# A linear-attention block with an MLP on one core: the first two tiles normalised in halves, and the ones column set in the normalised tiles

## The chip, the cores and the metric

The kernel runs on one core of one Trainium2 chip. A core has five engines with a queue each: TensorE (PE in the profile; PEld is its loading of weights, which overlaps the matmuls), VectorE (DVE), ScalarE (ACT), GpSimd (POOL) and SyncE (SP), which here issues all the DMA transfers. Each engine works through its own queue in order, and waits on semaphores for what the others produce. The metric is the device time in microseconds, the median of several runs; one execution was also profiled.

## The reference

All data is float32: 2048 tokens of 512 features, 32 heads of 16, a hidden layer of 1376.

```
xn  = (x - mean(x)) / sqrt(var(x) + 1e-5)
q, k, v = split(xn @ wqkv)                 # 32 heads
phi(t) = where(t > 0, t + 1, exp(t)) + 1e-6
kv  = sum over tokens of phi(k)^T v        # one 16 x 16 matrix per head
z   = sum over tokens of phi(k)
o   = phi(q) kv / (phi(q) z + 1e-6)
out = x + o @ wo + relu(xn @ w1 + b1)^2 @ w2 + b2
```

## The kernel before

The 2048 tokens are 16 tiles of 128. Every float32 product is made of three matmuls on numbers split into a high part (a copy in the matmul type, made by ScalarE) and a low part (the rest, by subtraction): high x high, high x low, low x high.

The work comes in stages. First, for each tile: statistics (`statistics`: `bn_stats` and `bn_aggr` on VectorE), the inverse root of the variance (`roots`: a logarithm and an exponential on ScalarE, then three small Newton instructions on VectorE at the head of `normalise`, lines 234 to 236), and the normalised tile `xp` (line 242). Tiles 0 to 7 are turned by TensorE (`turned_pe`, four 128 x 128 transposes into one bank); tiles 8 to 15 are regrouped by 32 small DMA transfers (`regroup`, `moves`) and turned by VectorE. The turned tile is split (`transposed` returns `high` on ScalarE, `low` on VectorE and `keep_t`, which stores tiles 0 to 7 for later), and the keys are projected with the weights `wk`, which are loaded in four parts of 128 rows and split by `heads_k` (ScalarE) and `rests_k`.

The keys go through `phi_k`, and `parts` splits the result into `pk`. The normalised tile itself is split by `tokens` into `tok`: high by ScalarE, low by GpSimd (line 116). Then `kx(i)` adds tok^T pk to four banks, twelve matmuls of 512 columns per tile: first the high-high products of the four column blocks, then high-low, then low-high, for tiles 0 to 7. The last column of the normalised tile isn't needed (the rows of a normalised tile sum to zero, so the value weights are taken less their last row), and it is overwritten with ones, so that the last row of the sum is z. In the kernel before, GpSimd does that after the split: line 314 copies a one and a zero from `consts` into the last column of the high and of the low part of `tok`.

After this stage come queries, attention, and the two layers of the MLP, which the change doesn't touch.

The schedule is manual: each engine's queue holds its instructions in the order in which the program text issues them, and only the semaphores between engines are found automatically. The start is written out by hand from line 479 on: statistics and roots of tiles 0 and 1, normalisation of tile 0, weight part 0, the turning of tile 0, weight part 1, normalisation of tile 1, a one-element GpSimd copy (line 490) that makes the load of tiles 4 to 7 wait for tile 1's factor, and so on; then the order of the projection's steps for tiles 0 and 1 (`some` does the products with the high weights, `rest` those with the low weights). From line 602 a loop goes over tiles 2 to 15: in iteration i come the projection of tile i, the turning of tile i + 1, `phi_k(i)`, `parts(i)`, `tokens(i + 1)` and `kx(i - 1)`. Ahead of the first tile stand eleven small matmuls on zeros in TensorE's queue (line 453).

The lines that set the order around the change:

```
two_tiles = statistics(0), statistics(1)
for t in two_tiles:
    roots(*t)
normalise(*two_tiles[0])
heads_k(0)
high, low, keep0 = transposed(0)
high()
heads_k(1)
normalise(*two_tiles[1])
```

Of the kernel before, what the change touches and what calls it, by code (L numbers as in the profile page):

```python
# [7 lines left out]
F32 = mybir.dt.float32  # L8
F32R = mybir.dt.float32r
AF = mybir.ActivationFunctionType  # L10
OP = mybir.AluOpType
AX = mybir.AxisListType

P = 128
# [4 lines left out]
def kernel(  # L19
# [29 lines left out]
    nc = tc.nc  # L49
    xf = x.rearrange("b s d -> (b s) d")  # L50
    of = out.rearrange("b s d -> (b s) d")
    S, D = xf.shape
    F = w1.shape[1]
    NT = S // P
    NJ = D // P
# [4 lines left out]
    NPE = 2 * TB  # L60
# [8 lines left out]
    keep = ctx.enter_context(tc.tile_pool(name="keep", bufs=1))  # L69
# [5 lines left out]
    def bank(name, tag="ps"):  # L75
        return psum.tile([P, 512], F32, name=name, tag=tag)

    def w512(name, tag, bufs):
        return work.tile([P, 512], F32, name=name, tag=tag, bufs=bufs)
# [8 lines left out]
    def two(name):  # L88
        return keep.tile([P, 2, 512], F32, name=name, tag=next_tag("x"))

    def four(name, tag, dt=F32, pool=None):
        return (pool or work).tile([P, TB, 512], dt, name=name, tag=tag)

    def pair(name):
        return keep.tile([P, 2, 512], F32R, name=name, tag=next_tag("pair"))

    def f32(ap):
        return ap.bitcast(F32)

    def gjc(ap):  # L100

        return ap.rearrange("p (j g c) -> p g j c", j=NJ, g=NJ)
# [3 lines left out]
    def copy(eng, o, i, bias=0.0):  # L106
        if eng == "act":
            nc.scalar.activation(o, i, AF.Copy, bias=bias)  # L108
        elif bias:
            ENG[eng].tensor_scalar(o, i, bias, None, op0=OP.add)  # L110
        else:
            ENG[eng].tensor_copy(o, i)

    def split(h, l, src, eh, el):
        copy(eh, h, src)
        ENG[el].tensor_tensor(out=l, in0=src, in1=f32(h), op=OP.subtract)  # L116
# [14 lines left out]
    def both(name, tags, dt=F32R, pool=keep):  # L131
        return [pool.tile([P, NJ, D], dt, name=f"{name}{u}", tag=t) for u, t in zip("hl", tags)]

    wk = both("wk", ("A0", "A1"))
# [11 lines left out]
    heads = work.tile([P, P], F32, name="heads", tag="heads")  # L146
    b1s = keep.tile([P, NF], F32, name="b1s")
    zb = keep.tile([P, D], F32, name="zb")
    consts = keep.tile([P, 3, 1], F32R, name="consts")
    one_zero, eps = consts[:, :2], f32(consts[:, 2])  # L150

    xr, xp, xg, tok, pk, kp = {}, {}, {}, {}, {}, {}

# [53 lines left out]
    def group(*tiles):  # L207
        return tiles, *(small.tile([P, 3, k], F32, name=f"{n}{tiles[0]}", tag=n) for n, k in (("st", 6), ("mv", 2), ("y", 3)))

    def measure(g, *ks):  # L210

        tiles, st, mv, _ = g
        for k in ks or range(len(tiles)):
            nc.vector.bn_stats(st[:, k, :], xr[tiles[k]])  # L214
            nc.vector.bn_aggr(mv[:, k, :], st[:, k, :])

    def statistics(*tiles):
        g = group(*tiles)
        measure(g)
        return g  # L220

    def roots(tiles, st, mv, y):

        n = len(tiles)
        nc.scalar.activation(y[:, 1, :n], mv[:, :n, 1], AF.Ln, bias=eps)
        nc.scalar.activation(y[:, 0, :n], y[:, 1, :n], AF.Exp, scale=-0.5)

    def normalise(tiles, st, mv, y):

        n = len(tiles)  # L230
        var = mv[:, :n, 1]
        y0, u, r = (y[:, k, :n] for k in range(3))

        nc.vector.scalar_tensor_tensor(u, var, 1e-5, y0, op0=OP.add, op1=OP.mult)
        nc.vector.scalar_tensor_tensor(u, u, -0.5, y0, op0=OP.mult, op1=OP.mult)
        nc.vector.scalar_tensor_tensor(r, u, 1.5, y0, op0=OP.add, op1=OP.mult)
        for k, i in enumerate(tiles):
            o, src = xp[i], xr[i]
            if i >= NPE:

                o, src = o.rearrange("p g (j c) -> p g j c", j=NJ), gjc(src)
            nc.vector.tensor_scalar(o, src, mv[:, k, 0:1], r[:, k:k + 1], op0=OP.subtract, op1=OP.mult)  # L242
            if i in groups:
                regroup(*groups[i])

    def regroup(src, G):

        for r in range(NJ):
            for g in range(NJ):
                moves.append((G[32 * g:32 * (g + 1), r], src[32 * r:32 * (r + 1), g]))  # L250
        return G
# [8 lines left out]
    def turn(o, G):  # L260

        nc.vector.transpose(o.rearrange("p j (r t) -> p r j t", r=NJ),  # L262
                            G.rearrange("p r (j c) -> p r j c", j=NJ))

    def slot(i):
        return slice((i % TB) * P, (i % TB + 1) * P)

    def cols(i):

        return xsb[(i // TB + 1) % 2]  # L270

    def turned_pe(i):
        p = bank(f"pt{i}", "acc" if i < 3 else "ps")
        for j in range(NJ):
            at_j = slice(j * P, (j + 1) * P)
            nc.tensor.transpose(p[:, at_j], xp[i][:, at_j], ident)  # L276
        return p.rearrange("p (j t) -> p j t", j=NJ)

    def transposed(i, t=None):

        b, at = i // TB, slot(i)
        if i < NPE:
            t = t or turned_pe(i)
        else:
            t = xT[b][:, :, at]
            turn(t, xg[i])
        h, l = (x[:, :, at] for x in cols(i))

        def high():
            nc.scalar.activation(h, t, AF.Copy)  # L290

        def low():
            nc.vector.tensor_tensor(out=l, in0=t, in1=f32(h), op=OP.subtract)

        def keep_t():
            if i < NPE:
                k = w512(f"t{i}", "p", 6).rearrange("p (j t) -> p j t", j=NJ)
                copy("act", k, t)
                nc.sync.dma_start(xTd[b][:, :, at], k)

        return high, low, keep_t

    def run(*what):
        for f in what:
            f()

    def tokens(i):
        tok[i] = pair(f"tok{i}")
        h, l = tok[i][:, 0], tok[i][:, 1]
        src = xp[i]  # L310
        if i >= NPE:
            h, l, src = gjc(h), gjc(l), src.rearrange("p g (j c) -> p g j c", j=NJ)
        split(h, l, src, "act", "pool")
        nc.gpsimd.tensor_copy(tok[i][:, :, D - 1:], one_zero)  # L314

    def phi(ps, p, mid=lambda: None, late=lambda: None):

# [6 lines left out]
    def project(i, ps, w, steps, first=True, last=True):  # L324

        for n, (j, u, v) in enumerate(steps):
            nc.tensor.matmul(ps, lhsT=cols(i)[u][:, j, slot(i)], rhs=w[v][:, j, :], start=first and n == 0,  # L327
                             stop=last and n == len(steps) - 1)
# [99 lines left out]
    t, rk = two("x0"), four("rk", "r0")  # L428
    for i in range(2):
        load_x(i, t[:, i:i + 1])  # L430
    def load_k(*js):
        for j in js:
# [4 lines left out]
    nc.gpsimd.memset(ident, 0.0)  # L437
    nc.gpsimd.affine_select(out=ident, in_=ident, compare_op=OP.not_equal, fill=1.0, base=0,
                            pattern=[[-1, P]], channel_multiplier=1)
    nc.gpsimd.memset(f32(one_zero[:, 0]), 1.0)  # L440
    nc.gpsimd.memset(f32(one_zero[:, 1]), 0.0)
    nc.gpsimd.memset(heads, 1.0)
    h3 = heads.rearrange("p (h d) -> p h d", d=D // H)
    for sign, base in ((1, 0), (-1, D // H - 1)):
# [25 lines left out]
    def heads_k(*js):  # L470
        for j in js:
            copy("act", wk[0][:, j, :], rk[:, j])
# [4 lines left out]


    pks = [bank(f"pk{i}") for i in range(3)]
    two_tiles = statistics(0), statistics(1)  # L480
    for t in two_tiles:
        roots(*t)
    normalise(*two_tiles[0])
    heads_k(0)
    high, low, keep0 = transposed(0)
    high()
    heads_k(1)
    normalise(*two_tiles[1])

    nc.gpsimd.tensor_copy(x4[:, 0, :1], two_tiles[1][3][:, 2, :1])  # L490
    load_x(4, x4)
# [10 lines left out]
    keep1()  # L502
    rests_k("dve", 1)
    normalise(*third)
    rests_k("dve", 3)
    fourth = statistics(3)

    def some(i, u, js, first=False):
        project(i, pks[i], wk, [(j, u, 0) for j in js], first, False)

    def rest(j):
        for i in range(2):
            project(i, pks[i], wk, [(j, 0, 1)], False, j == NJ - 1)

    for j in (0, 1):
        some(0, 0, (j,), j == 0)
    some(0, 1, (0, 1))
    some(1, 0, (0, 1), True)
    some(0, 0, (2,))
    some(0, 1, (2,))  # L520
    some(1, 0, (2,))
    some(1, 1, (0, 1, 2))
    for i in range(2):
        for u in range(2):
            some(i, u, (3,))
    rest(0)
    rest(2)
    high, low, keep2 = transposed(2)
    high()
    low()  # L530
    rest(1)
    rest(3)
    load_x(8, x8[:, :2])
# [5 lines left out]
    phi_k(0, pks[0])  # L539
    measure(soon, 0)  # L540
    tokens(0)
    parts(0)
    keep2()
    roots(*fourth)
    normalise(*fourth)
    phi_k(1, pks[1])
    measure(soon, 1)
    tokens(1)
    parts(1)
    measure(soon, 2)  # L550
# [51 lines left out]
    for i in range(2, NT):  # L602
# [12 lines left out]
        k = NPE if i + 1 == NPE else i + 2  # L615
# [13 lines left out]
        if i == 2:  # L629
            tokens(2)  # L630
# [108 lines left out]
    for n in range(2):  # L739
# [212 lines left out]
        f = NF - 2  # L952
# [31 lines left out]
        for e, f in enumerate(waiting[:-2]):  # L984
# [7 lines left out]
            if e:  # L992
                do(w2next, 2)
                if e + 8 < NF:
                    g = waiting[e + 8]
# [65 lines left out]
```

## Time and profile before

| | |
|---|---|
| median of 3 runs | 425.09 us (425.08 to 425.21) |
| the profiled execution | 425.03 us, its span 423.3 us |
| granted TensorE clock | 1.000 |
| busy: TensorE, VectorE, ScalarE, GpSimd | 417.3, 299.0, 248.6, 33.3 us |
| TensorE's wait for its first transposes after the warm-up | 0.8 us |
| weight loads of `kx` waiting for line 314 | 1.0 us in two waits |

The span is the time from the first to the last instruction; what a run takes lies 1.7 us above it. A row of the timeline or of the chain begins with the start and the duration in microseconds; then come engine, line, operation, and the tile written "<-" the tiles read. A bracket at the end is the idle time of the engine before the instruction and what ended it. Matmuls are pipelined: a row's duration is longer than the distance to the next. Rows that merge several instructions give their count (x4).

### The profile page before, as it was taken

What the parts mean: (1) busy time and instruction counts of PE and PEld (TensorE: products, weight loads), DVE (VectorE), ACT (ScalarE), POOL (GpSimd) and SP (SyncE); (2) the same over time, 40 slices, a digit from 0 to 9 for tenths busy, and PEclk for the clock granted to TensorE, in tenths of its full rate; (3) what the DMA queues carried; (4) which work ended last, traced back from release to release, by engine and by line L of the source; (5) the groups of instructions that cost most, each with busy time, mean ns of one, the idle gap of its engine ahead of it and who ended that gap; (6) DMA issues with size and microseconds to landing.
All of it is one profiled execution on the core that took longest, in us unless ns stands there. A gap on an engine that the chain in (4) does not pass through costs nothing.

```text
span 423.3 us, 5387 instructions
## 1 busy us (share of the span) xinstructions
PE 417.3 (99%) x1868; PEld 344.0 (81%) x1868; DVE 299.0 (71%) x537; ACT 248.6 (59%) x441; POOL 33.3 (8%) x52
## 2 busy tenths in 40 slices
PE   7999999999999999999999999999999999999996
PEld 6788888888887888888888888888888888888885
DVE  6897788855678877777579475586967667677253
ACT  5766667645467777565438362666667665537140
POOL 3342333330000000000000000000000000000000
PEclk9999999999999999999999999999999999999999
DMA  7853437000412231547014652501120654023602
GB/s 251 274 159 83 106 104 228 18 0 2 112 50 71 80 91 35 197 79 272 0 37 125 189 193 80 140 0 50 51 74 25 200 101 150 0 93 87 162 0 99
DMA packets 42754, 43.02 MB, mean 102 GB/s; under 512 B 5828, under 2 KB 28612, under 8 KB 42472
## 3 DMA queue, kind: packets, MB, share of 16 engines
q1 hardware_dynamic: 42728, 42.69, 33.9%
q8 instruction: 14, 0.23, 0.2%
q14 instruction: 12, 0.10, 0.1%
HBM read 30.09 MB, written 6.29 MB: 86 GB/s over the span
## 4 chain that ended last, share of the span: by engine, by line
PE 97%; DVE 1%; DMA 1%; POOL 0%; ACT 0%; issue 0%; POOLq 0%
PE acc L127 39%; PE b L411 23%; PE kx L346 10%; PE pq L327 10%; PE pk L327 10%; PE pz L127 1%; PE b L127 1%; PE pkv L722 1%; PE pt L276 1%; PE pm L127 1%; DMA x<-in_A_x_dram 1%; PE end L127 0%; DVE st L214 0%; POOL tok L116 0%; DVE xp L242 0%; ACT k L320 0%
## 5 line engine op out<-in xcount | busy, mean ns | idle before, releaser
L127 PE MATMUL acc<-w2r,s 128*128 128x512 f32 x498 | 116.6, 389 | 0.0
L127 PEld LDWEIGHTS acc<-w2r,s 128*128 128x128 f32 x498 | 93.5, 188 | 19.6
L411 PE MATMUL b<-T,aop 128*128 128x512 f32 x240 | 59.6, 389 | 0.0
L411 PEld LDWEIGHTS b<-T,aop 128*128 128x128 f32 x240 | 45.0, 188 | 9.4
L346 PE MATMUL kx<-pk,tok 128*128 128x512 f32 x192 | 47.3, 394 | 0.1
L346 PEld LDWEIGHTS kx<-pk,tok 128*128 128x128 f32 x192 | 35.4, 188 | 8.2 <-POOL tok L314 1.0
L127 PE MATMUL acc<-mh,aT 128*128 128x512 f32 x128 | 41.0, 396 | 0.0
L127 PEld LDWEIGHTS acc<-mh,aT 128*128 128x128 f32 x128 | 24.0, 188 | 5.7
L119 DVE TENSOR_TENSOR w2r<-r,w2r 128x512 fp32r<-128x512 f32 x32 | 21.9, 684 | 7.2 <-ACT w2r L108 6.4
L411 PE MATMUL b<-xs0h,aop 128*128 128x512 f32 x80 | 26.4, 391 | 0.0
L116 POOL TENSOR_TENSOR tok<-xp,tok 128x512 fp32r<-128x512 f32 x16 | 22.1, 1380 | 53.6 <-ACT tok L108 53.6
L116 DVE TENSOR_TENSOR s<-c,s 128x512 fp32r<-128x512 f32 x20 | 13.9, 693 | 16.7 <-ACT s L108 16.7
L127 PE MATMUL acc<-ml,aT 128*128 128x512 f32 x64 | 25.3, 395 | 0.0
L108 ACT ACTIVATE w2r<-r 128x512 fp32r<-128x512 f32 x32 | 20.0, 624 | 9.0 <-PE acc L127 8.7
L199 POOL MEMSET r<- 32x512 f32 x3 | 1.6, 522 | 279.1 <-DMA g<-q 145.1
L322 DVE SCALAR_TENSOR_TENSOR q<-pq,q 128x512 f32<-128x512 f32 x16 | 11.0, 689 | 17.0 <-ACT q L320 17.0
L852 DVE TENSOR_TENSOR res<-acc,res 128x512 f32<-128x512 f32 x16 | 11.0, 692 | 14.8 <-PE acc L127 14.8
L108 ACT ACTIVATE aop<-S 128x512 fp32r<-128x512 f32 x20 | 12.6, 629 | 14.6 <-DVE S L651 9.4
L318 ACT ACTIVATE q<-pq 128x512 f32<-128x512 f32 x16 | 9.5, 591 | 19.7 <-PE pq L327 19.7
L108 ACT ACTIVATE aT<-at 128x512 fp32r<-128x512 f32 x16 | 9.9, 631 | 17.3 <-DVE at L262 17.3
L318 ACT ACTIVATE k<-pk 128x512 f32<-128x512 f32 x16 | 9.5, 594 | 16.6 <-PE pk L327 16.5
L411 PEld LDWEIGHTS b<-xs0h,aop 128*128 128x128 f32 x80 | 15.0, 188 | 3.4 <-ACT rz L399 0.3
(184 smaller groups left out, 816.5 us busy)
## 6 DMA issues: line engine op xcount, KB each, us to landing
r<-in_B_w_dram SPq DMA_DIRECT2D x49, 256.0 KB, 3.0
res<-in_A_x_dram SPq DMA_DIRECT2D x8, 512.0 KB, 5.3
g<-q SPq DMA_DIRECT2D x64, 64.0 KB, 2.1
out_dram<-res SPq DMA_DIRECT2D x15, 256.0 KB, 2.0
x<-in_A_x_dram SPq DMA_DIRECT2D x5, 512.0 KB, 4.8
xTd<-t SPq DMA_DIRECT2D x8, 256.0 KB, 3.1
rq<-in_A_wqkv_dram SPq DMA_DIRECT2D x8, 256.0 KB, 5.8
xg<-xp SPq DMA_DIRECT2D x32, 64.0 KB, 2.0
```

The source lines that it names most:

```text
L108: nc.scalar.activation(o, i, AF.Copy, bias=bias)
L116: ENG[el].tensor_tensor(out=l, in0=src, in1=f32(h), op=OP.subtract)
L119: nc.vector.tensor_tensor(out=l, in0=src, in1=f32(h), op=OP.subtract)
L127: nc.tensor.matmul(ps, lhsT=a[u], rhs=b[v], start=first and n == 0, stop=last and n == 2)
L276: nc.tensor.transpose(p[:, at_j], xp[i][:, at_j], ident)
L318: nc.scalar.activation(p, ps, AF.Relu, scale=-1.0)
L322: nc.vector.scalar_tensor_tensor(p, ps, 0.0, p, op0=OP.max, op1=OP.add)
L327: nc.tensor.matmul(ps, lhsT=cols(i)[u][:, j, slot(i)], rhs=w[v][:, j, :], start=first and n == 0, stop=last and n == len(steps) - 1)
L346: nc.tensor.matmul(kxp[c], lhsT=tok[i][:, u, c * P:(c + 1) * P], rhs=pk[i][:, v], start=i == 0 and (u, v) == first, stop=i == NT - 1 and ( ...
L411: nc.tensor.matmul(ps, lhsT=a[u][:, j * P:(j + 1) * P], rhs=b[v][:, j, :], start=first and j == 0 and n == 0, stop=last and j == 1 and n == 2,
L722: nc.tensor.matmul(ps[:, at], lhsT=wvs[:, c, at], rhs=kxs[c // 2][:, c % 2, at], start=c == 0 and j == 0, stop=c == NJ - 1 and j == NJ - 1 ...
L852: nc.vector.tensor_tensor(out=r[:, a:z], in0=ps, in1=r[:, a:z], op=OP.add)
```

## The change

- Tiles 0 and 1 are no longer normalised by `normalise`. `first_roots` computes -0.5 (var + 1e-5) on VectorE as soon as the variance is there, and issues the logarithm and the exponential; `first_norm` then needs two small Newton instructions instead of three, and normalises the tile in two instructions of 256 columns each instead of one of 512.
- VectorE's order becomes: statistics of tile 0, its half factor, `bn_stats` of tile 1, the Newton steps and halves of tile 0, `bn_aggr` of tile 1, its half factor, and later its Newton steps and halves. Before, all statistics came first.
- ScalarE's order becomes: roots of tile 0, weight part 0, roots of tile 1, high part of tile 0, weight part 1. Before, both roots came ahead of weight part 0.
- TensorE does the first product of tile 0 (weight part 0) between the transposes of tile 0 and those of tile 1, instead of after both.
- The ones are written into `xp` by a GpSimd memset of one column (`ones`): for tiles 0 to 7 directly after the tile's transposes, for tiles 8 to 15 at the end of `tokens` of the tile before. The copy after the split and the tile `consts`, with its two memsets at the start, are gone; `eps` gets a tile of its own.

```diff
-    consts = keep.tile([P, 3, 1], F32R, name="consts")
-    one_zero, eps = consts[:, :2], f32(consts[:, 2])
+    eps = keep.tile([P, 1], F32, name="eps")
...
+    def first_roots(g):
+        u = keep.tile([P, 1], F32, name=f"half{g[0][0]}")
+        nc.vector.tensor_scalar(u, g[2][:, 0, 1:], 1e-5, -0.5, op0=OP.add, op1=OP.mult)
+        roots(*g)
+        return u
+
+    def first_norm(g, u):
+
+        (i,), st, mv, y = g
+        y0, t, r = y[:, 0, :1], y[:, 1, :1], y[:, 2, :1]
+        nc.vector.scalar_tensor_tensor(t, u, y0, y0, op0=OP.mult, op1=OP.mult)
+        nc.vector.scalar_tensor_tensor(r, t, 1.5, y0, op0=OP.add, op1=OP.mult)
+        for k in range(2):
+            at = slice(k * D // 2, (k + 1) * D // 2)
+            nc.vector.tensor_scalar(xp[i][:, at], xr[i][:, at], mv[:, 0, :1], r, op0=OP.subtract, op1=OP.mult)
...
             nc.tensor.transpose(p[:, at_j], xp[i][:, at_j], ident)
+        ones(i)
         return p.rearrange("p (j t) -> p j t", j=NJ)
...
+    def ones(i):
+
+        nc.gpsimd.memset(xp[i][:, D - 1:] if i < NPE else xp[i][:, NJ - 1, P - 1:], 1.0)
+
...
         split(h, l, src, "act", "pool")
-        nc.gpsimd.tensor_copy(tok[i][:, :, D - 1:], one_zero)
+        if NPE <= i + 1 < NT:
+            ones(i + 1)
...
-    nc.gpsimd.memset(f32(one_zero[:, 0]), 1.0)
-    nc.gpsimd.memset(f32(one_zero[:, 1]), 0.0)
...
-    two_tiles = statistics(0), statistics(1)
-    for t in two_tiles:
-        roots(*t)
-    normalise(*two_tiles[0])
...
+    two_tiles = group(0), group(1)
+    measure(two_tiles[0])
+    half = first_roots(two_tiles[0])
+    nc.vector.bn_stats(two_tiles[1][1][:, 0, :], xr[1])
+    first_norm(two_tiles[0], half)
+    nc.vector.bn_aggr(two_tiles[1][2][:, 0, :], two_tiles[1][1][:, 0, :])
     heads_k(0)
+    half = first_roots(two_tiles[1])
     high, low, keep0 = transposed(0)
     high()
     heads_k(1)
-    normalise(*two_tiles[1])
+    some(0, 0, (0,), True)
+    first_norm(two_tiles[1], half)
...
-    for j in (0, 1):
-        some(0, 0, (j,), j == 0)
+    some(0, 0, (1,))
     some(0, 1, (0, 1))
     some(1, 0, (0, 1), True)
     some(0, 0, (2,))
```

More of the change, by code (lines that the diff above doesn't have):

```diff
@@ L479, with some, rest @@
     pks = [bank(f"pk{i}") for i in range(3)]
-    two_tiles = statistics(0), statistics(1)
-    for t in two_tiles:
-        roots(*t)
-    normalise(*two_tiles[0])
+    def some(i, u, js, first=False):
+        project(i, pks[i], wk, [(j, u, 0) for j in js], first, False)
+    def rest(j):
+        for i in range(2):
+            project(i, pks[i], wk, [(j, 0, 1)], False, j == NJ - 1)
+    two_tiles = group(0), group(1)
[4 more added lines that the diff above has]
+    nc.vector.bn_aggr(two_tiles[1][2][:, 0, :], two_tiles[1][1][:, 0, :])
     heads_k(0)
+    half = first_roots(two_tiles[1])
     high, low, keep0 = transposed(0)
@@ L506 @@
     fourth = statistics(3)
[L508 to L513, printed above, removed]
-    for j in (0, 1):
-        some(0, 0, (j,), j == 0)
+    some(0, 0, (1,))
     some(0, 1, (0, 1))
```

## The prediction

> **What bounds the kernel now.** First the page's busy times and chain, to see which engine sets the end; then the chain in order of time, to see where that engine is not yet dense; then the timelines of VectorE, ScalarE and GpSimd over the first 24 us, because everything that the diff touches lies there.
>
> ```profile
> PE 417.3 (99%) x1868; PEld 344.0 (81%) x1868; DVE 299.0 (71%) x537; ACT 248.6 (59%) x441; POOL 33.3 (8%) x52
> PE 97%; DVE 1%; DMA 1%; POOL 0%; ACT 0%; issue 0%; POOLq 0%
> ```
>
> TensorE is busy 417.3 of 423.3 us and makes 97% of the chain. The change removes no matmul, so it can only alter when the dense stream begins and how long it is held up before it runs without a gap. The chain shows where that is:
>
> ```profile
> 7.42 0.65 PE pt L276 x4
> 8.07 0.23 PE pk L327
> ...
> 8.31 4.62 PE pk L327 x19
> 12.93 0.44 PE pt L276 x4
> ...
> 14.10 0.61 ACT k L318
> ...
> 15.96 1.30 POOL tok L116
> ...
> 17.32 0.54 POOL tok L314
> ...
> 17.91 2.34 PE kx L346 x9
> 20.25 0.44 PE pt L276 x4
> 20.68 3.01 PE kx L346 x12
> 23.69 2.72 PE pk L327 x12
> ```
>
> From 23.69 on, twelve matmuls take 2.72 us, 0.227 each, and this repeats: the stream is dense. Before that there are three losses. (1) The 19 matmuls from 8.31 end at 12.93; 19 x 0.227 = 4.31, so the first of them really ran at 8.62, 0.3 behind its weight load (a load that waits exposes about 0.3 us; it starts 0.06 after what it waited for, here a weight part that ended at 8.25, quoted below). Counting back from 12.93, the products of these twenty started at: third (first low part of tile 0) 8.84, fifth (first of tile 1) 9.30, seventh (first with weight part 2) 9.75. (2) The first kx: nine matmuls from 17.91 take 2.34 instead of 2.04. (3) The second kx: 3.01 instead of 2.72. Whatever the new code makes of these is the whole effect; the profiled execution took 425.03 us (span 423.3 and 1.7 around it), the median is 425.09.
>
> **The change, part by part: the first tiles.** The rows of VectorE, ScalarE and the loads that set the start:
>
> ```profile
> 4.33 0.18 DVE L215 BATCH_NORM_AGGREGATE mv<-st 128x2 f32<-128x6 f32 x1
> 4.43 0.67 DVE L214 BATCH_NORM_STATS2 st<-x 128x6 f32<-128x512 f32 x1
> ...
> 5.23 0.13 DVE L234 SCALAR_TENSOR_TENSOR y<-mv,y 128x1 f32<-128x1 f32 x1
> ...
> 5.58 0.16 DVE L236 SCALAR_TENSOR_TENSOR y<-y 128x1 f32<-128x1 f32 x1
> 5.78 0.55 DVE L242 TENSOR_SCALAR xp<-x,mv,y 128x512 f32<-128x512 f32 x1
> 6.24 0.15 DVE L234 SCALAR_TENSOR_TENSOR y<-mv,y 128x1 f32<-128x1 f32 x1
> ...
> 6.82 0.55 DVE L242 TENSOR_SCALAR xp<-x,mv,y 128x512 f32<-128x512 f32 x1
> 7.77 0.69 DVE L293 TENSOR_TENSOR xs1l<-pt,xs1h 128x512 fp32r<-128x512 f32 x1 [0.41 <-ACT xs1h L290]
> ```
> ```profile
> 5.35 0.29 ACT L225 ACTIVATE y<-mv,consts 128x1 f32<-128x1 f32 x1 [0.27 <-DVE y L234]
> 5.67 0.20 ACT L226 ACTIVATE y<-y 128x1 f32<-128x1 f32 x1
> 5.79 0.61 ACT L108 ACTIVATE wkh<-rk 128x512 fp32r<-128x512 f32 x1
> 7.14 0.60 ACT L290 ACTIVATE xs1h<-pt 128x512 fp32r<-128x512 f32 x1 [0.74 <-PE pt L276]
> 7.63 0.62 ACT L108 ACTIVATE wkh<-rk 128x512 fp32r<-128x512 f32 x1
> 8.15 0.59 ACT L290 ACTIVATE xs1h<-pt 128x512 fp32r<-128x512 f32 x1
> 8.63 1.15 ACT L108 ACTIVATE wkh<-rk 128x512 fp32r<-128x512 f32 x2
> ```
> ```profile
> L367 DVE TENSOR_SCALAR den<-den 128x32 f32<-128x32 f32 x16 | 2.9, 181 | 0.6
> ```
> ```profile
> 1.72 1.85 SPq L433 DMA_DIRECT2D rk<-in_A_wqkv_dram  x4
> ```
> ```profile
> DMA to landing us min/median/max: 3.7/3.7/3.7
> ```
>
> Pitch: an instruction that depends on the one before starts 0.02 to 0.04 after its end; one that doesn't starts about 0.09 before that end (5.78 + 0.55 = 6.33, the next at 6.24). A half of the normalisation (128x256) has no row. Bounds: half the elements at one per 1.04 ns leave 0.28; a doubled rate, which the 0.46 us from 5.78 to 6.24 speaks for (less than 512 x 1.04 ns), leaves 0.41. I take 0.35, on the line between the same operation over 32 columns (0.18) and over 512 (0.55).
>
> By the Trainium skill, "VectorE: DVE Perf Modes", section "Side-by-side", such an operation in fp32 moves two elements a cycle behind about 150 cycles: an estimate of 0.29 for a half, with which the end would be 424.6. The same rule gives 0.42 for the whole, where this trace has 0.55; so the trace decides.
>
> Tile 0. The half factor, 0.14, goes between the two statistics: 4.53 to 4.67, second statistics 4.59 to 5.26, the two remaining Newton steps 5.18 to 5.53, first half 5.57 to 5.92, second 5.83 to 6.18 (whole before: 6.33). The last two of four transposes are left behind the second half; four take 0.44, so 0.2 drops out of the 0.70 from the end at 7.37 to 8.07: transposes done at 6.68 instead of about 7.1.
>
> Tile 1 pays. Its aggregate now stands behind tile 0's halves: 6.09 to 6.27 instead of 5.13. The logarithm and the exponential follow (0.04 later, then 0.32 + 0.20): 6.31 to 6.83. The weight part now ahead of them, landing at 1.72 + 3.7 = 5.42, runs 5.46 to 6.07 and is out of the way. The high part of tile 0 starts 6.75 instead of 7.14. On VectorE: Newton steps 6.87 to 7.22, halves 7.26 to 7.61 and 7.52 to 7.87, against 7.37 before: 0.50 later. Transposes done 7.87 + 0.70 - 0.2 = 8.37 (8.07 before); the product moved ahead of them needs the high part of tile 0 (7.35) and is done in the gap. High part of tile 1: 8.41 to 9.01. Its first product: load 9.07, run 9.36, against 9.30: +0.06. Weight part 2 starts 0.48 after that high part: 8.89 to 9.50, load 9.56, run 9.85, against 9.75: +0.10. The low part of tile 0 starts 7.79, level with 7.77. So the early start of tile 0 isn't kept, and the stream is 0.10 late: term one, +0.10, between -0.10 (half 0.28) and +0.35 (half 0.41).
>
> **The ones.** Rows of the kx stage:
>
> ```profile
> 16.82 0.98 DVE L335 SCALAR_TENSOR_TENSOR pk<-k,pk 128x512 fp32r<-128x512 f32 x1
> ...
> 20.26 0.98 DVE L335 SCALAR_TENSOR_TENSOR pk<-k,pk 128x512 fp32r<-128x512 f32 x1
> ```
> ```profile
> 1.33 0.10 POOL L440 MEMSET consts<- 128x1 f32 x1
> ...
> 17.32 0.53 POOL L314 CAST tok<-consts 128x2 fp32r<-128x2 f32 x1
> 19.41 1.29 POOL L116 TENSOR_TENSOR tok<-xp,tok 128x512 fp32r<-128x512 f32 x1 [1.55 <-ACT tok L108]
> ```
> ```profile
> 17.91 1.91 PEld L346 LDWEIGHTS kx<-pk,tok 128*128 128x128 f32 x9 [0.56 <-POOL tok L314]
> ...
> 21.35 1.92 PEld L346 LDWEIGHTS kx<-pk,tok 128*128 128x128 f32 x9 [0.40 <-POOL tok L314]
> ```
>
> Three weight loads of each early kx pass, the fourth waits for the copy of the ones column: its columns end with that column. Without the copy the fourth waits for nothing new; the fifth is the first that reads the low part of pk, which ends at 17.80 and 21.24, just 0.05 to 0.06 before the copy did. So the wait doesn't vanish: it moves one matmul on. Per kx that is 0.227 + 0.05 = 0.28 saved. It isn't saved twice: the second kx hangs on the chain that ends at 21.24, which starts from the projection's end at 14.10 and runs through ScalarE, VectorE and GpSimd whatever the first kx did. Term two: -0.28 by 23.69. The ends are 0, if some other operand ties, and -0.79, both waits (0.5 and 0.29) gone.
>
> Why the low part doesn't come sooner: it takes 0.98 instead of the 0.69 that its kind takes elsewhere, and ends 0.54 after GpSimd's subtraction (17.26 and 20.70) both times, so the subtraction holds it, not the copy. The Trainium skill, "SBUF — State Buffer", section "Who interferes with whom", has an exclusive lock here, the second to issue blocking fully; by it the copy waited for VectorE and its removal frees nothing there, as the equal 0.54 shows. Were it shared instead, the low part would end some 0.1 earlier and the sum would be -0.28 for the whole change.
>
> Costed at nothing: sixteen one-column memsets on GpSimd, 0.1 each like those removed at the start (0.10 at 1.33), hidden because GpSimd is busy 8%; without that cover the first subtraction would be 0.1 late, and the low part with it. For tiles 3 to 7 each stands behind its tile's transposes and ahead of its own subtraction, for tiles 8 to 15 behind the regrouping loads, more than an iteration ahead of use. The other fourteen copies: their kx were dense, nothing to gain. The load of tiles 4 to 7 hangs on a GpSimd copy of tile 1's factor, which is 0.44 later and has a memset before it; SyncE's order is kept, and the tiles are first read after 16.
>
> Sum: +0.10 - 0.28 = -0.18; 425.03 - 0.18 = 424.85, with the median 0.06 above the profiled execution **424.9**.
>
> **Rivals.**
>
> ```profile
> 6.93 0.48 POOL L490 COPY x<-y 128x1 f32<-128x1 f32 x1 [4.31 <-DVE y L236]
> ```
> ```profile
> L314 POOL CAST tok<-consts x16: 187/396/534, 17.3 to 92.9; 128x2 fp32r<-128x2 f32 x16
> ```
>
> Slower: GpSimd's copy gets between tile 1's halves. Before, it issued 0.11 after the normalisation began, took 0.48 where a copy of two columns takes 0.19 at best, and ended with it: it was held. Now there is an end of the first half to slip into, at 7.61; the second half would run 7.80 to 8.15, 0.28 later, and the stream with it: 0.10 + 0.28 - 0.28 = +0.10, about 425.2, or 425.5 with halves of 0.41. It decides from a second half that ends past 8.05. Against it: the second half is queued first. 0.20.
>
> No gain in kx: another operand ties at the fourth load, so only term one is left: 425.2. For it: the low part of pk was only 0.05 ahead; against: the fourth matmul doesn't read it. 0.10.
>
> Both kx waits vanish and tile 1 isn't late: -0.79 - 0.35 = 423.9. It needs the low part of pk 0.3 sooner; the equal 0.54 speaks against. 0.09.
>
> Weight part 0 lands late: ScalarE now waits for it ahead of tile 1's logarithm. It decides past 5.8 (row: 5.42), and each microsecond then costs one; before, at 5.79, it was there without a wait. 426 would need a landing at 6.8. 0.06.
>
> **How the numbers follow.** My forecast, between 424.3 and 425.0, has 0.55. The range 424.3 to 425.5 holds it and the rivals at 425.2. What two runs of this kernel can tell apart is about 0.2%, 0.85 us: faster by that (under 424.2) only the third rival, 0.09; slower (over 425.9) the last, 0.06; the rest, 0.85, is the same.
>
> **What would show it.** Right: the halves of the second tile end near 7.9, later than 7.37; ScalarE's second high part starts near 8.4; the fifth kx load, not the fourth, is held, by VectorE's L335-line instruction; the subtraction is followed by no copy; TensorE dense 0.2 earlier than 23.69. Wrong: a half outside 0.28 to 0.41, GpSimd's copy between the halves, or kx passing without a wait.

## The result and the profile after

| | before | after |
|---|---|---|
| median | 425.13 us (424.78 to 425.54, 19 runs) | 425.94 us (425.71 to 426.35, 19 runs) |
| ratio after / before | | 1.0018, 95% interval 1.0012 to 1.0025 |
| the profiled execution: time, span | 425.03, 423.3 us | 425.71, 423.6 us |
| median span; median time outside the span | 423.5; 1.72 us (33 further runs, median 425.19) | 423.9; 2.08 us |

The change costs 0.81 us, where the prediction had a gain of about 0.2. The gain in `kx` came as forecast; the start cost much more than priced; and 0.36 us lies outside the span, which the prediction had taken as constant. The profiled execution of the kernel after is one of its shortest: its spans go from 423.6 to 424.2.

From the page of the kernel after, the busy times and the chain by engine:

```profile
PE 418.2 (99%) x1868; PEld 345.3 (82%) x1868; DVE 299.6 (71%) x539; ACT 248.3 (59%) x441; POOL 28.4 (7%) x50
PE 99%; DVE 0%; ACT 0%; issue 0%
```

The same 1868 matmuls; GpSimd is busy 4.9 us less, since memsets of 1.5 us stand in place of copies of 5.8 us and some others got shorter or went. TensorE now has 99% of the chain, but not because it is denser: the chain goes back through the warm-up (below). The chain of the kernel after in order of time, up to the end of the second `kx`:

```profile
2.97 3.63 PE warm L472 x17
6.60 0.49 PE pt L291 x4
7.09 0.02 issue
7.11 0.61 ACT xs1h L306
7.71 0.04 issue
7.76 0.50 PE pk L348
8.26 0.44 PE pt L291 x4
8.69 4.70 PE pk L348 x19
...
17.52 2.93 PE kx L367 x12
20.45 0.44 PE pt L291 x4
20.88 2.99 PE kx L367 x12
23.87 0.23 PE pk L348
```

Read the middle. The warm-up lasts to 6.60 here (before, to 5.62) and holds tile 0's transposes, whose tile is ready at 6.13; they end at 7.09, ScalarE makes the high part, the product moved ahead follows at 7.76, and tile 1's transposes start only when that product ends, at 8.26. They end at 8.69; before, at 8.07, although here the first tile landed 0.26 us earlier (first statistics at 3.34; before, 3.60). VectorE, ScalarE and TensorE's weight loads at the start of the kernel after (start, duration, then what; the bracket is idle time and what ended it):

```profile
5.39 0.74 DVE L241 TENSOR_SCALAR xp<-x,mv,y 128x256 f32<-128x256 f32 x2
6.04 0.18 DVE L511 BATCH_NORM_AGGREGATE mv<-st 128x2 f32<-128x6 f32 x1
6.25 0.15 DVE L229 TENSOR_SCALAR half<-mv 128x1 f32<-128x1 f32 x1
6.87 0.22 DVE L237 SCALAR_TENSOR_TENSOR y<-half,y 128x1 f32<-128x1 f32 x1 [0.47 <-ACT y L225]
7.32 0.73 DVE L241 TENSOR_SCALAR xp<-x,mv,y 128x256 f32<-128x256 f32 x2
```
```profile
5.79 0.63 ACT L108 ACTIVATE wkh<-rk 128x512 fp32r<-128x512 f32 x1 [0.97 <-DMA rk<-in_A_wqkv_dram]
6.33 0.28 ACT L224 ACTIVATE y<-mv,eps 128x1 f32<-128x1 f32 x1
8.73 0.60 ACT L306 ACTIVATE xs1h<-pt 128x512 fp32r<-128x512 f32 x1 [0.50 <-PE pt L291]
```
```profile
7.76 0.19 PEld L348 LDWEIGHTS pk<-wkh,xs1h 128*128 128x128 f32 x1 [0.93 <-ACT xs1h L306]
7.89 0.56 PEld L291 LDWEIGHTS pt<-ident,xp 128*128 128x128 f32 x4
...
9.38 0.30 PEld L348 LDWEIGHTS pk<-wkh,xs1h 128*128 128x128 f32 x2 [0.37 <-ACT xs1h L306]
...
17.27 0.76 PEld L367 LDWEIGHTS kx<-pk,tok 128*128 128x128 f32 x4 [0.18 <-ACT pk L108]
18.33 1.69 PEld L367 LDWEIGHTS kx<-pk,tok 128*128 128x128 f32 x8 [0.30 <-DVE pk L356]
...
20.71 0.76 PEld L367 LDWEIGHTS kx<-pk,tok 128*128 128x128 f32 x4
21.75 1.69 PEld L367 LDWEIGHTS kx<-pk,tok 128*128 128x128 f32 x8 [0.28 <-DVE pk L356]
```

Two halves take 0.73 to 0.74, where the one instruction took 0.55: 0.41 each, 0.33 apart. Tile 1 is normalised at 8.05, 4.71 after the first statistics began; before, 7.37 and 3.77. And in the last four rows each `kx` has four weight loads and is held at the fifth, by VectorE's low part of `pk`, just as forecast. That low part takes as long as before (0.98):

```profile
17.29 0.99 DVE L356 SCALAR_TENSOR_TENSOR pk<-k,pk 128x512 fp32r<-128x512 f32 x1
...
20.73 0.97 DVE L356 SCALAR_TENSOR_TENSOR pk<-k,pk 128x512 fp32r<-128x512 f32 x1
```

### The profile page after: what moved, and what is told of

The parts are those of the page before. It is cut to its first block, busy times and chain, and to the rows that moved or that the text cites. A ratio compares the mean times of both kernels' runs of the same rounds, so it can differ in the third digit from the quotient of the medians.

```text
span 423.6 us, 5383 instructions
## 1 busy us (share of the span) xinstructions
PE 418.2 (99%) x1868; PEld 345.3 (82%) x1868; DVE 299.6 (71%) x539; ACT 248.3 (59%) x441; POOL 28.4 (7%) x50
## 4 chain that ended last, share of the span: by engine, by line
PE 99%; DVE 0%; ACT 0%; issue 0%
PE acc L127 39%; PE b L432 23%; PE pk L348 10%; PE kx L367 10%; PE pq L348 10%; PE pz L127 1%; PE b L127 1%; PE warm L472 1%; PE pkv L744 1%; PE pt L291 1%; PE pm L127 1%; PE end L127 0%; ACT xs1h L306 0%; DVE zb L447 0%; DVE res L874 0%
```

## The experiments

Each kernel ran beside runs of the kernel before on the same chip, whose medians were 425.19 (for ones alone, start alone, statistics first, whole normalisation), 425.27 (product behind, both undone, warm-up of 8, no new tiles) and 425.11 (the memsets and the order of `kx`). None changes what is computed. The median span of these three sets of the kernel before was 423.5, 423.6 and 423.4, so spans from different sets compare to some 0.2. "Outside" is the time less the span.

| kernel | median, us | ratio to before, 95% interval | median span | outside | records in VectorE's queue |
|---|---|---|---|---|---|
| before | 425.13 | | 423.5 | 1.72 | 689 |
| after | 425.94 | 1.0012 to 1.0025 | 423.9 | 2.08 | 696 |
| ones alone | 424.94 | 0.9982 to 0.9999 | 423.2 | 1.73 | 692 |
| start alone | 425.94 | 1.0014 to 1.0038 | 424.25 | 1.70 | 693 |
| after, statistics first | 425.83 | 1.0006 to 1.0023 | 423.9 | 1.97 | 694 |
| after, whole normalisation | 425.73 | 1.0000 to 1.0018 | 423.8 | 1.95 | 694 |
| after, product behind | 425.80 | 1.0005 to 1.0023 | 423.7 | 2.08 | 696 |
| after, statistics first and product behind | 425.37 | 0.9992 to 1.0011 | 423.4 | 1.94 | 694 |
| ones, warm-up of 8 | 425.57 | 0.9993 to 1.0011 | 423.9 | 1.71 | 692 |
| after, no new tiles | 425.84 | 1.0004 to 1.0021 | 423.8 | 2.06 | 696 |
| ones, 2 memsets more | 424.95 | 0.9982 to 1.0000 | 423.0 | 1.955 | 694 |
| ones, 4 memsets more | 425.18 | 0.9988 to 1.0007 | 423.1 | 2.065 | 696 |
| ones, 20 memsets more | 425.09 | 0.9989 to 1.0007 | 423.4 | 1.695 | 712 |
| ones, other order of `kx` | 424.83 | 0.9980 to 0.9997 | 423.1 | 1.73 | 692 |

(The last column counts all records of VectorE's queue in the trace, with the waits and register instructions that the page leaves out.)

**The two parts apart.** The theory: the ones give their 0.28 and the start costs more than 0.10. The rival: the ones gave nothing, or less. (The edits here and below are cut short. This one is against the kernel before; the others are against the kernel after, or against the ones alone where the text says so.)

```diff
+    def ones(i):
+        nc.gpsimd.memset(xp[i][:, D - 1:] if i < NPE else xp[i][:, NJ - 1, P - 1:], 1.0)
...
-        nc.gpsimd.tensor_copy(tok[i][:, :, D - 1:], one_zero)
+        if NPE <= i + 1 < NT:
+            ones(i + 1)
```

> The kernel before with the ones part alone: the memsets in the normalised tiles in place of the copies after the split; the start is that of before. Theory A (the loss lies in the start, the ones are a gain): TensorE's stream is dense 0.28 us earlier than before, the span is 0.28 shorter, and the time is 424.85 if what lies outside the span stays at 1.7. Theory B (the ones part costs, by what it does to the code behind the stream or to GpSimd): 425.3 or more, with the 0.36 us that the changed kernel has outside its span.

The other kernel is the reverse: the new start, with the copy of the ones kept.

```diff
-        ones(i)
         return p.rearrange("p (j t) -> p j t", j=NJ)
...
-        if NPE <= i + 1 < NT:
-            ones(i + 1)
+        nc.gpsimd.tensor_copy(tok[i][:, :, D - 1:], one_zero)
```

> The changed kernel with the copies of before in place of the memsets: the start alone. Theory A: the fifth product of the projection runs 0.45 later than before and nothing of it is won back in kx, so the span is 0.45 longer: 425.6, or 425.95 if the 0.36 outside the span comes with the start. Theory B (the start is neutral): 425.1.

The ones alone: 424.94 against 425.19, so 0.25 faster. The start alone: 425.94 against 425.19, 0.75 slower, and none of it outside the span. The median is the 425.95 of the expectation by chance only: that was made of 0.45 in the span and 0.36 outside, and the run has 0.75 and nothing. The chain of the start alone:

```profile
1.72 4.36 DMA rk<-in_A_wqkv_dram
6.08 0.02 issue
6.11 0.63 ACT wkh L108
6.74 0.19 ACT y L225
...
7.16 0.49 ACT xs1h L306
7.65 0.04 issue
7.70 0.50 PE pk L343
8.20 0.67 PE pt L292 x4
8.87 4.70 PE pk L343 x19
...
18.55 2.34 PE kx L362 x9
20.89 0.44 PE pt L292 x4
21.32 2.99 PE kx L362 x12
```

Weight part 0, which now stands ahead of tile 1's roots, took 4.36 to land here (3.7 was the row that the prediction used; the fourteen profiles have 3.4 to 4.7 for this transfer, so one row could not price it). VectorE in the same kernel:

```profile
3.62 0.69 DVE L214 BATCH_NORM_STATS2 st<-x 128x6 f32<-128x512 f32 x1 [2.13 <-DMA x<-in_A_x_dram]
...
6.32 0.17 DVE L508 BATCH_NORM_AGGREGATE mv<-st 128x2 f32<-128x6 f32 x1
...
7.19 0.22 DVE L238 SCALAR_TENSOR_TENSOR y<-half,y 128x1 f32<-128x1 f32 x1 [0.51 <-ACT y L226]
...
7.64 0.74 DVE L242 TENSOR_SCALAR xp<-x,mv,y 128x256 f32<-128x256 f32 x2
```

The last half ends at 8.38. Tile 1's four transposes take 0.67 behind the product's end at 8.20, where four without a wait take 0.44: so the last half sets their end, 8.87, and the product's end would have set it 0.23 sooner, at 8.64. The second `kx` ends at 24.31 instead of 23.69. In the spans the two parts add up: +0.75 - 0.3 = +0.45, and after has +0.4.

**What in the start costs.** One theory: tile 1's statistics and roots, behind tile 0's halves, are late. A second: the product ahead of tile 1's transposes holds them. A third: a half costs more than half. One is undone at a time, then two together. The figure to watch, beside the span, is how long after the start of the first statistics tile 1's transposes are done, since the first tile's landing varies by 0.4 from profile to profile: before and with the ones alone 4.47, start alone 5.25, after 5.35.

```diff
-    half = first_roots(two_tiles[0])
-    nc.vector.bn_stats(two_tiles[1][1][:, 0, :], xr[1])
-    first_norm(two_tiles[0], half)
-    nc.vector.bn_aggr(two_tiles[1][2][:, 0, :], two_tiles[1][1][:, 0, :])
-    heads_k(0)
+    half0 = first_roots(two_tiles[0])
+    measure(two_tiles[1])
     half = first_roots(two_tiles[1])
+    first_norm(two_tiles[0], half0)
+    heads_k(0)
```

> The changed kernel with both tiles' statistics and roots ahead of tile 0's normalisation, as before the change; halves, short Newton step, product order and ones stay. If the late aggregate of tile 1 is what delays its first product: tile 1's halves end near 7.4 instead of 8.05, the fifth product runs 0.4 earlier than in the changed kernel, 425.5. If it is the product put ahead of tile 1's transposes, or the warm-up that still runs: within 0.15 of the changed kernel, 425.9.

No gain in the span: 423.9. VectorE's second pair of halves and TensorE in this kernel:

```profile
7.11 0.73 DVE L241 TENSOR_SCALAR xp<-x,mv,y 128x256 f32<-128x256 f32 x2
```
```profile
7.93 0.50 PE L348 MATMUL pk<-wkh,xs1h 128*128 128x512 f32 x1 [0.69 <-ACT xs1h L306]
8.26 0.60 PE L291 MATMUL pt<-ident,xp 128*128 128x128 f32 x4
```

Tile 1 is normalised at 7.84, 4.29 after the first statistics (after: 4.71), but its transposes wait for the product, which waits for tile 0's high part, and tile 0 is later now. They are done 5.31 after the first statistics: what VectorE gained, TensorE's order took.

```diff
-        for k in range(2):
-            at = slice(k * D // 2, (k + 1) * D // 2)
-            nc.vector.tensor_scalar(xp[i][:, at], xr[i][:, at], mv[:, 0, :1], r, op0=OP.subtract, op1=OP.mult)
+        nc.vector.tensor_scalar(xp[i], xr[i], mv[:, 0, :1], r, op0=OP.subtract, op1=OP.mult)
```

> The changed kernel with one normalising instruction of 512 columns for each of the two tiles instead of two of 256. If the halves cost more than they bring (two of them 0.74, one whole 0.55): tile 1 is normalised 0.35 earlier and the time is 425.6. If the early first half matters: later than the changed kernel, 426.1 or more.

One normalisation of 512 columns is 0.1 shorter in the span (423.8), and ends tile 1 4.28 after the first statistics instead of 4.71. So the halves are a loss on VectorE; in the time it isn't shown, since this kernel's spans go from 423.3 to 424.5. Tile 1's transposes are done 5.00 after the first statistics, and it is the product that holds them.

```diff
-    some(0, 0, (0,), True)
     first_norm(two_tiles[1], half)
...
-    some(0, 0, (1,))
+    for j in (0, 1):
+        some(0, 0, (j,), j == 0)
```

> The changed kernel with the first product of tile 0 behind the transposes of tile 1 again, as before the change. Theory P (that product, waiting for tile 0's high part and 0.5 long, holds tile 1's transposes): they end where tile 1's second half lets them, about 0.15 earlier here, since that half ends at 8.06 and they ended at 8.69; the span is 0.1 to 0.2 shorter than the changed kernel's 423.9. Rival (the late statistics of tile 1 alone set it): no change, 423.9.

With the product behind, 0.2 comes back (423.7), and now VectorE holds the transposes. VectorE and TensorE in this kernel:

```profile
7.57 0.74 DVE L241 TENSOR_SCALAR xp<-x,mv,y 128x256 f32<-128x256 f32 x2
```
```profile
8.04 0.76 PE L291 MATMUL pt<-ident,xp 128*128 128x128 f32 x4 [1.12 <-DVE xp L241]
8.55 0.71 PE L348 MATMUL pk<-wkh,xs1h 128*128 128x512 f32 x2
```

They are done 5.16 after the first statistics. The two causes lie side by side, each nearly as late as the other. So the next kernel has both edits, statistics first and the product behind:

> The changed kernel with both statistics and roots first and with the product behind tile 1's transposes: only halves, short Newton step and ones are left of the change. Alone, the statistics brought nothing (423.9). Theory P: with both undone tile 1's transposes end 0.5 earlier than with the statistics alone, the span is 423.4 to 423.5. Rival (the halves are what costs): span 423.7 or more.

Both undone give 0.5 of the span back (423.4), where one alone gave 0 or 0.2. Tile 1's transposes are done 4.78 after the first statistics, although in this profile the clock rose only at 7.46 and tile 0's transposes ran 0.21 apart instead of 0.11. What remains to the ones alone (423.2), 0.2, is left to the halves, the half factors and some 0.1 in the later stream (below); no run takes these apart.

**The warm-up.** In the profile of after, the eleven warm-up products (two matmuls each) end at 6.60, past the end of tile 0's normalisation at 6.13; before, at 5.62. In the trace the granted clock rises to full at 6.55 there and at 4.44 before, and until it rises a warm-up matmul takes about twice as long (0.213 from one to the next, then 0.112). A shorter warm-up, on the ones alone:

```diff
-    WARM = 11
+    WARM = 8
```

> The ones part alone, with 8 warm-up matmuls instead of 11. The warm-up ran to 5.6 or to 6.6, by when the granted clock rose, and in the second case the first transposes waited for it. If that wait is what it costs: it ends by 5.0 in every run, the slow half of the runs gains 0.2 to 0.3, span 423.1 against 423.2. If fewer matmuls let the clock rise a window (3.4 us) later: products at half speed, 424 or more.

Inconclusive as a gain, and a risk. Five of eleven executions had spans of 422.9 to 423.0, as short as the shortest of the ones alone (422.8 to 423.5); six had 423.9 to 424.5, and the median became 425.57. Its profile is of a short one: the warm-up ends at 5.32 and holds nothing. Why the others are longer no trace of them shows; that the warm-up was then too short to bring the clock up in time is only argued. The length of the warm-up isn't what makes after slow, since the start alone lost 0.75, and its profile, in which the clock rose at 4.48, has a span of 424.1 against the 423.3 of before with 4.44.

**The rest of the stream.** From the end of the second `kx` to TensorE's last matmul the traces have 396.54 to 396.58 in all six kernels that keep the half factors in two new tiles of one column, and 396.40 to 396.49 in the eight that don't have these tiles. The kernel that tests it puts the factor in an unused column of an existing tile:

```diff
-        u = keep.tile([P, 1], F32, name=f"half{g[0][0]}")
+        u = g[3][:, 2, 1:2]
```

> The changed kernel with the half factors kept in a spare column of the tile y instead of two tiles of their own; the same instructions in the same order. What two new tiles do to the addresses: if they cause the 0.13 us by which the dense stream is longer after 24 us and the 0.36 outside the span, those are back to 396.4 and 1.7, and the time is 425.45; if not, 425.94 as the changed kernel.

Its stream took 396.44, so the tiles cost some 0.1 in these traces; how, by where they put other tiles in SBUF or otherwise, no run shows. In the medians (425.84 against 425.94) this is within the interval and not shown. The time outside the span stayed at 2.06, so the tiles have no part in that.

**Outside the span.** The time outside the span is nearly the same in every execution of a program, and goes by program: 1.72 before, 2.08 after. A theory: it hangs on the length of VectorE's queue. The rivals: it hangs on what the added instructions do, or on GpSimd's work. The test adds only dead memsets of `eps` on VectorE, in the idle time before the first tile lands, to the ones alone:

```diff
-    nc.vector.memset(eps, 1e-5)
+    for _ in range(5):
+        nc.vector.memset(eps, 1e-5)
```

> The same with four more memsets, 696 instructions on VectorE, as in the changed kernel. Theory L: 2.08 outside the span, and so 425.3 with the span of the ones alone. Rival: 1.73 and 424.94.

With `range(3)` there are two more, with `range(21)` twenty more:

> The ones part alone, with two more one-column memsets of the same constant on VectorE at 1.5 us, where it waits for the first load: VectorE's queue has 694 instructions in the trace instead of 692. The time outside the span was 1.7 us with 689, 692 and 693 of them (before, ones, start), 1.95 with 694 (statistics first, whole) and 2.08 with 696 (changed kernel). Theory L (that length sets it): span 423.2 as with the ones alone, 1.95 outside it. Rival (the order of the start, or its code elsewhere, sets it): 1.73.

> The same with twenty more memsets, 712 instructions on VectorE, still done before the first load lands. If the time outside the span grows with each instruction past 693 (0.12 each): near 4. If it is a step that is passed once: 2.1 to 2.2. If it belongs to the start's order: 1.73.

Two memsets put 0.22 outside the span, four 0.33, and twenty none. None of the three expectations for twenty had a length that costs nothing again; its 1.73 was named for the start's order, which two and four memsets on the old start rule out. So it is the length, and a band of it that costs, as far as these lengths go: 689, 692 and 693 records have 1.70 to 1.73, the four kernels with 694 have 1.94 to 1.97, the four with 696 have 2.06 to 2.08, and 712 has 1.70. The last records of the trace are signals on one semaphore, after the span, in a fixed rhythm. The distances between the last six, in ns:

```
before (689)              24   98   38   35   46
after (696)               23  454   38   34   47
ones, 2 more (694)        23   99   38   34   47
ones, 4 more (696)        24  454   38   34   47
ones, 20 more (712)       23   99   38   34   47
```

With 696, one signal comes 0.36 later: that is what the kernel after has more outside its span. (With 694 the delay isn't in this row; where it lies, the traces don't show.) From the page of the kernel with twenty memsets, the row of the second instruction queue:

```profile
q14 instruction: 13, 0.11, 0.1%
```

All other kernels, after too, have one packet fewer:

```profile
q14 instruction: 12, 0.10, 0.1%
```

The additional packet, 8 KB of instructions, is fetched at 415.8 in the trace, within the span, where nothing waits for it. What this suggests, and no run shows directly: with 694 to 696 records the queue's last instructions fall just across the end of a fetched block, the next is fetched behind the end of the work, and the program waits for it; with 712 it is fetched early. The traces have no packets at all behind the span, so the late fetch itself is not seen. By the Trainium skill, "Runtime: NRT & Kernel Launch", section "Instruction fetch mechanics", each engine's instructions come in blocks through a queue of its own, and crossing a block's end is mostly hidden. The traces have instruction packets of 8 KB on one queue and of 16 KB on another, which agrees on the blocks, though a queue for each engine is not to be seen in them; if a crossing is the cause, it is not hidden here, at 0.24 to 0.36 us. With twenty memsets the last ended late, and the first statistics began at 3.93, so its span is no better than before.

**A version that beats before and after.** The ones alone, with the low-high products of tiles 0 to 7 ahead of the high-low ones, so that the low part of `pk` is needed four matmuls later:

```diff
-        order = (((1, 0),), ((0, 0), (0, 1))) if i >= NPE else (((0, 0),), ((0, 1),), ((1, 0),))
+        order = (((1, 0),), ((0, 0), (0, 1))) if i >= NPE else (((0, 0),), ((1, 0),), ((0, 1),))
```

> The ones part alone, with the products of kx for tiles 0 to 7 in the order high-high, low-high, high-low: the low part of pk is then read by the ninth matmul, not the fifth. If the low part of pk is all that holds the first two kx: they run 2.72 each, the dense stream begins 0.3 to 0.4 earlier, span 422.8, 424.55. If the low part of tok, now read by the fifth, comes no sooner: 424.94 as with the ones alone.

424.83, 0.28 faster than the runs of before beside it; from the ones alone (424.94) the intervals don't tell it apart, so only before and after are shown to be beaten. The mechanism is plain in TensorE's weight loads of this kernel:

```profile
17.24 2.59 PEld L351 LDWEIGHTS kx<-pk,tok 128*128 128x128 f32 x12 [0.18 <-ACT pk L108]
19.87 0.58 PEld L275 LDWEIGHTS pt<-ident,xp 128*128 128x128 f32 x4
20.68 2.59 PEld L351 LDWEIGHTS kx<-pk,tok 128*128 128x128 f32 x12 [0.23 <-ACT pk L108]
```

Twelve loads in a row: the wait for the low part is gone. What comes forward is little, because the wait for the high part of `pk`, which lay in front of it, grows.

## Why the prediction was wrong, point by point

**Term one, the start, +0.10: this step failed; it was mis-sized.** It measured +0.75. The place was right: tile 1 pays for tile 0, and tile 0's early start isn't kept. The forecast had tile 1's transposes done at 8.37, that is 4.77 after the first statistics; the start alone took 5.25. Its rows, each less the 3.62 of its first statistics and beside the forecast less 3.60:

- Tile 1's aggregate: 2.70, forecast 2.49, so 0.21 late. Tile 0's two halves take 0.74 instead of 0.61, its Newton steps some 0.05 more than 0.35. "I take 0.35" was the error: the half is 0.41 and the next starts 0.33 behind it, the upper bound, for which the 0.46 from 5.78 to 6.24 spoke. The straight line went through two different forms: the row of 32 columns adds one constant (line 367), the normalisation takes two values for each row. From 32 to 256 columns it comes to 1.03 ns a column, from 256 to 512 to 0.53. The estimate of 0.29 from the Trainium skill ("VectorE: DVE Perf Modes", section "Side-by-side") has the rate right, as the 0.13 between the two pitches (0.46 and 0.33) shows, and a fixed part that is 0.12 too short here.
- Tile 1's Newton steps start at 3.57, forecast 3.27: 0.30 late, 0.09 more than the aggregate. That is weight part 0, which landed at 6.08, not 5.42, and ran ahead of the roots.
- The last half ends at 4.76, forecast 4.27: 0.49 late, with 0.13 more from tile 1's own halves and the rest from its Newton steps.

So 0.10 + 0.49 = 0.59, and with the 0.14 of the later stream (396.54 against 396.40) it is 0.73: the measured +0.75. The traces say the same from end to end: the second `kx` ends 0.62 later than before and the span is 0.76 longer. The bound of +0.35 had the halves at 0.41, and none of the rest. Of the 0.65 by which the term was short, the halves are 0.26; the short instructions ahead of them are 0.14, weight part 0 is 0.09 and the later stream 0.14.

"The product moved ahead of them ... is done in the gap" was a second weak step. By the forecast's own numbers (high part at 7.35, product to 7.90, four transposes in 0.44) the transposes would end at 8.34, 0.03 ahead of the 8.37 that VectorE allowed: a tie that went unsaid. In after it went the other way. The warm-up held tile 0's transposes to 7.09, where the forecast, moved by 0.26 for the earlier tile, had 6.42; so the product ended at 8.26 and tile 1's transposes at 8.69, while the last half, at 8.05, would have allowed about 8.55 (0.49 behind it, as in the start alone). Because of the tie neither edit alone gave much, and both gave 0.5; with both undone tile 1's transposes came 4.78 after the first statistics. That this is the forecast's own figure is chance, for its order was another.

**The 1.7 outside the span, taken as constant: this failed too.** It became 2.08, +0.36, by the length of VectorE's queue.

**Term two, the ones, -0.28: right.** -0.25 in the median and -0.3 in the span. The traces agree: from the start of the nineteen products to the end of the second `kx` it is 15.38 before (8.31 to 23.69) and 15.11 with the ones alone (8.41 to 23.52), 0.27 less. The fifth load, not the fourth, is held, by the low part of `pk`, for 0.30 and 0.28; it takes 0.99 and 0.97 as before (0.98), so the copy had not held it. The memsets are hidden.

**The sum.** +0.75 - 0.25 + 0.36 = +0.86; measured, +0.81. All of the miss is in term one and outside the span.

**The rivals.** GpSimd's copy between the halves: it cost nothing. The rival's sign, a second half that ends past 8.05, did come up (8.38 in the start alone), but because the Newton steps ahead of it began late. In after it took 0.18 from 7.35 on, beside the first half, and the halves still took 0.73; with the statistics first it ran across their border (7.41 to 7.59, the second half from 7.43), and again they took 0.73. No gain in `kx`: excluded by the ones alone. Both waits of `kx` gone: no; removing the second wait too, by the order, gave 0.1 at most. Weight part 0 late: it happened (ScalarE idle for 0.97 in after), but as the aggregate was late too it cost 0.09 in the start alone, a tenth of a microsecond where the rival wanted a whole one. That the product holds tile 1, and that the warm-up holds tile 0, were no rivals at all.

**What would show it.** Second halves near 7.9: 8.05, and 4.71 behind the first statistics instead of 4.27. The second high part near 8.4: 8.73. The fifth load held, and no copy behind the subtraction: right. Dense 0.2 earlier than 23.69: 23.87, later. A half within 0.28 to 0.41: at its end.

## What to carry to other kernels

An instruction that is moved forward in an engine's order stands in front of all that follows it: write down by how much its own operands are early enough, for a margin of some hundredths is a coin's toss. When two late arrivals lie close together at one place, undo them together as well as one by one, since each hides the other's gain. And compare the time outside the span between versions: a few instructions more on one queue were worth as much here as a stall in the kernel, and dead instructions that cost no engine time can show whether that is so.

## What the runs showed of the hardware that was not expected

- The time outside the span goes by the number of records in VectorE's queue, in a band: 1.70 to 1.73 us up to 693, 1.94 to 1.97 at 694, 2.06 to 2.08 at 696, and 1.70 again at 712.
- The clock rises at a time that varies from one profile to the next, 4.36 to 7.76 in the thirteen with the same warm-up begun at 1.53. By the Trainium skill, "TensorE: Matmul & The Clock Gate", section "Part 1: The HAM clock gate (the "warmup" mystery)", the window of 3.4 us that decides runs free of the kernel; these rises lie within 3.4 us of each other, which agrees.
- Two more tiles of one column went with a stream that is 0.1 us longer in all six profiles that have them (396.54 to 396.58, against 396.40 to 396.49 in eight without).
